# Sliding-window attention: 36 groups on 128-key blocks against 16 batches of 64-key blocks on smaller array tiles

## The chip, the cores and the metric

One core of one Trainium2 chip. The time is that of one execution on the device, in microseconds (us). Single durations are from profiled executions. All comparisons are between runs of the normal ("fast") state.

The engines: PE is TensorE (matmuls), PEld its weight loads, ACT is ScalarE, DVE is VectorE, POOL is GpSimd, SP the engine that issues the transfers. "L358" is line 358 of a kernel's file. PSUM is the memory that matmuls write to, in banks. A tile of the array is the part of its rows and columns that one matmul uses ("32*64" in the views); to change the tiling is to go on with tiles of another shape. A pair is a matmul with its weight load. The granted clock is the share of its full rate at which PE was let run.

## The reference

Two attention blocks over the same 2048 x 1024 input, 32 heads of 32, mixed by a gate. Block A is linear attention and is not touched. Block B lets each query see 8 keys, two positions apart:

```python
W, dil = 8, 2
idx = pos[:, None] - off[None, :]           # off = 0, 2, 4 .. 14
mask = idx >= 0
logits = jnp.einsum("bhsd,bhswd->bhsw", q, kg) * scale
logits = jnp.where(mask[None, None, :, :], logits, -1e9)
attn = _softmax(logits, axis=-1)
o = jnp.einsum("bhsw,bhswd->bhsd", attn, vg)
...
return g * a + (1 - g) * b
```

The kernels split positions into even and odd ("parity"), so that the 8 keys of a query are neighbours. A block of keys then serves a run of queries, with a band mask on exponentiated scores.

## The kernel before

PE's order is fixed by hand. In the attention stage the units of a long stream are the K and Q projections of block B (512-column matmuls, eight to a PSUM bank), and attention groups are dropped between them. Four tiles of 128 keys by 112 (or 128) queries, four heads each, make one group. There are 36 groups.

```python
def kq_units(c, kqt):
    ...                                     # 8 matmuls into a bank of ps_pj (2 banks), then its copy:
        after = (64 * c + 16 * b + 8 * which + 8 - 67) % (512 / 36)
        (nc.vector.tensor_copy if 0 <= after < 4 else nc.scalar.copy)(
            out=kqt[:, which, cols], in_=st["pj"][:])

def scores(g):                              # 16 matmuls, 32 rows x 128 columns of the array each
    for c, t, q0, w, k0 in tiles:
        for i in range(4):
            r = slice(32 * i, 32 * i + 32)
            nc.tensor.matmul(s4[:, i, o:o + w], lhsT=kqts[c][r, 0, k0:k0 + P],
                             rhs=kqts[c][r, 1, q0:q0 + w], start=True, stop=True)
    ...                                     # exponential on ACT, mask product on DVE, in two halves

def pv(g):                                  # 16 matmuls on the whole array, 33 columns (V and a 1)
    for b in range(2):
        for i in range(4):
            for tt in range(2 * b, 2 * b + 2):
                nc.tensor.matmul(oB[b][:, tt - 2 * b, i, :], lhsT=pt[:, i * W_ + o:i * W_ + o + P],
                                 rhs=V[:, t, c * 4 + i, :], start=True, stop=True)
    ...                                     # reciprocal, product on DVE; transposed by DMA
# cut: groups are placed every 512/36 units; pv 18 units after its scores
```

Note the choice in `kq_units`: the projection copy that falls just after a score group goes to DVE, because ACT then has two long exponentials to do.

The softmax here doesn't subtract the row's maximum and nothing guards it: scores larger than these inputs give would overflow.

## Time and profile before

| | before |
|---|---|
| median of the runs given first | 487.87 us (487.74 to 490.22) |
| PE busy, share of the span | 99% |
| attention stage, first projection matmul to first output matmul | 153.46 us |
| of it the 576 projection matmuls at 0.2157 us | 124.24 us |
| the rest: what attention costs PE | 29.2 us |

The last rows come from the start times of the matmuls in the trace. First, busy time per engine and the chain that ended last, from the page of the kernel before:

```profile
PE 480.5 (99%) x3444; PEld 227.0 (47%) x3444; DVE 281.0 (58%) x533; ACT 187.4 (39%) x283; POOL 15.9 (3%) x33
...
PE 98%; DMA 1%; SPq 1%; ACT 0%; issue 0%; ACTq 0%
PE kq_ps L339 23%; PE d_ps L454 21%; PE p_ps L258 11%; PE g_ps L200 11%; PE pk_ps L152 11%; PE p_ps L296 9%; PE q_ps L296 3%; PE oB L390 3%; PE s L365 2%; PE q_ps L454 1%; DMA WkA<-in_A_wqkv_dram 1%; PE kv_ps L220 0%; PE p_ps L246 0%; SPq L95 0%; SPq L98 0%; SPq L99 0%
```

A chain that is 98% PE says that only PE time counts: whatever ACT or DVE saves is worth nothing unless PE waits for them. Attention itself (oB and s) is only about 5% of the chain.

One group in the timeline of PE, kernel before (start, duration, engine, line, operation, output<-input, array rows*columns, count):

```profile
301.78 0.81 PE L339 MATMUL kq_ps<-xT,WkB 128*128 128x512 bf16 x3
302.52 0.38 PE L365 MATMUL s<-kqt 32*128 32x128 bf16 x16
302.83 1.04 PE L339 MATMUL kq_ps<-xT,WkB 128*128 128x512 bf16 x4
303.71 0.56 PE L390 MATMUL oB<-V,PT 128*128 128x33 bf16 x16
304.12 0.38 PE L339 MATMUL kq_ps<-xT,WkB 128*128 128x512 bf16 x1
```

Durations overlap, so read the starts. In the trace the last projection matmul before the scores starts at 302.209. A next one would follow 0.216 later, but the first score matmul comes at 302.520: 0.095 us lost. 15 more starts follow, then 0.14 us pass before the projections go on. PV needs no such pauses: 16 starts, 25.3 ns apart, 0.405 us.

### The profile page before, as it was taken

The page shows a single profiled execution, that of the slowest core. Times are in us where ns is not written, and L with a number is a line of the kernel's source. Part 1 is how long each engine was busy: PE and PEld are TensorE (multiplying, and loading weights), DVE is VectorE, ACT ScalarE, POOL GpSimd, SP SyncE. Part 2 cuts the span into 40 slices and gives each one's busy share as a digit, 9 for nine tenths or more (in the row PEclk, how much of TensorE's full clock was granted, in tenths as well). Part 3 has the DMA queues.
Part 4 walks back from the last instruction along what each step waited for, and adds up shares of the span by engine and source line. Part 5 has one row for each costly group of instructions (what it writes and reads, how often), then busy time and mean ns, then how long its engine had stood idle before and what let it go on. Part 6 is the DMA issues. An engine that isn't in the chain of part 4 may idle for free.

```text
span 486.2 us, 8390 instructions
## 1 busy us (share of the span) xinstructions
PE 480.5 (99%) x3444; PEld 227.0 (47%) x3444; DVE 281.0 (58%) x533; ACT 187.4 (39%) x283; POOL 15.9 (3%) x33
## 2 busy tenths in 40 slices
PE   7999999999999999999999999999999999999997
PEld 4444444445444444444444445544445444444444
DVE  1766689992429999995466556656654596000000
ACT  1333321111633333332666666666565332212121
POOL 3000001411000000000000000000000000000000
PEclk9999999999999999999999999999999999999999
DMA  8999960001522223354011161111173833111101
GB/s 194 171 291 369 348 207 0 0 1 36 190 76 93 72 71 93 95 158 131 11 30 31 30 121 27 38 30 32 31 172 78 198 88 86 34 43 34 43 33 45
DMA packets 80182, 46.57 MB, mean 96 GB/s; under 512 B 53520, under 2 KB 74128, under 8 KB 80144
## 3 DMA queue, kind: packets, MB, share of 16 engines
q1 hardware_dynamic: 80144, 46.04, 34.9%
q8 instruction: 27, 0.44, 0.4%
q14 instruction: 11, 0.09, 0.1%
HBM read 21.23 MB, written 7.34 MB: 59 GB/s over the span
## 4 chain that ended last, share of the span: by engine, by line
PE 98%; DMA 1%; SPq 1%; ACT 0%; issue 0%; ACTq 0%
PE kq_ps L339 23%; PE d_ps L454 21%; PE p_ps L258 11%; PE g_ps L200 11%; PE pk_ps L152 11%; PE p_ps L296 9%; PE q_ps L296 3%; PE oB L390 3%; PE s L365 2%; PE q_ps L454 1%; DMA WkA<-in_A_wqkv_dram 1%; PE kv_ps L220 0%; PE p_ps L246 0%; SPq L95 0%; SPq L98 0%; SPq L99 0%
## 5 line engine op out<-in xcount | busy, mean ns | idle before, releaser
L375 ACT ACTIVATE PT<-s 128x896 bf16<-128x896 f32 (+1 forms) x72 | 63.0, 926 | 24.5 <-PE s L365 24.5
L339 PE MATMUL kq_ps<-xT,WkB 128*128 128x512 bf16 x256 | 65.3, 379 | 0.0
L339 PE MATMUL kq_ps<-xT,WqB 128*128 128x512 bf16 x256 | 64.8, 379 | 0.0
L376 DVE TENSOR_TENSOR PT<-PT,mask 128x896 bf16<-128x896 bf16 (+1 forms) x72 | 44.6, 623 | 26.6 <-ACT PT L375 26.6
L258 PE MATMUL p_ps<-WvB,xT 128*128 128x512 bf16 x256 | 57.9, 379 | 0.0
L152 PE MATMUL pk_ps<-WkA,xT 128*128 128x512 bf16 x256 | 56.0, 379 | 1.3 <-DMA WkA<-in_A_wqkv_dram 0.8
L454 PE MATMUL d_ps<-WoA,pqT 128*128 128x512 bf16 (+1 forms) x248 | 56.9, 372 | 0.0
L454 PE MATMUL d_ps<-WoB,OBT 128*128 128x512 bf16 (+1 forms) x248 | 56.9, 372 | 0.0
L200 PE MATMUL g_ps<-pk,xrow 128*128 128x512 bf16 x256 | 55.4, 379 | 0.0
L140 DVE TENSOR_SCALAR e<-e 128x512 f32<-128x512 f32 x64 | 28.1, 438 | 41.8 <-ACT e L139 41.8
L459 ACT ACTIVATE osb<-d_ps,omg 128x512 bf16<-128x512 f32 (+1 forms) x31 | 20.9, 673 | 76.5 <-PE d_ps L454 73.7
L296 PE MATMUL p_ps<-WqA,xT 128*128 128x512 bf16 x192 | 43.4, 379 | 0.0
L344 ACT CAST kqt<-kq_ps 128x512 bf16<-128x512 f32 x48 | 28.2, 587 | 31.8 <-PE kq_ps L339 31.6
L152 PEld LDWEIGHTS <-xT 128*128 128x128 bf16 x256 | 24.9, 98 | 32.2 <-issue 1.6
L454 PEld LDWEIGHTS <-pqT 128*128 128x128 bf16 x264 | 25.8, 98 | 29.5
L454 PEld LDWEIGHTS <-OBT 128*128 128x128 bf16 x264 | 25.8, 98 | 29.3
L200 PEld LDWEIGHTS <-xrow 128*128 128x128 bf16 x256 | 25.0, 98 | 30.2
L258 PEld LDWEIGHTS <-xT 128*128 128x128 bf16 x256 | 24.6, 98 | 30.0 <-issue 0.9
L296 PEld LDWEIGHTS <-xT 128*128 128x128 bf16 x256 | 24.3, 98 | 28.5
L139 ACT ACTIVATE e<-pk_ps 128x512 f32<-128x512 f32 x32 | 19.0, 597 | 42.0 <-PE pk_ps L152 42.0
L339 PEld LDWEIGHTS <-WqB 128*128 128x128 bf16 x256 | 22.9, 97 | 24.7
L339 PEld LDWEIGHTS <-WkB 128*128 128x128 bf16 x256 | 22.6, 97 | 24.1
(56 smaller groups left out, 394.1 us busy)
## 6 DMA issues: line engine op xcount, KB each, us to landing
xrow<-in_A_x_dram SPq DMA_DIRECT2D x4, 1024.0 KB, 12.3
out_dram<-osb SPq DMA_DIRECT2D x31, 128.0 KB, 1.9
pqd<-tmp SPq DMA_DIRECT2D x12, 256.0 KB, 2.0
WvA<-in_A_wqkv_dram SPq DMA_DIRECT2D x2, 1024.0 KB, 15.0
WoA<-in_A_wo_dram SPq DMA_DIRECT2D x2, 1024.0 KB, 12.7
WvB<-in_B_wqkv_dram SPq DMA_DIRECT2D x2, 1024.0 KB, 12.5
WqA<-in_A_wqkv_dram SPq DMA_DIRECT2D x2, 1024.0 KB, 9.7
WkB<-in_B_wqkv_dram SPq DMA_DIRECT2D x2, 1024.0 KB, 6.6
```

Source lines behind the costliest of these rows:

```text
L139: nc.scalar.activation(out=e[:], in_=pj[:], func=ACT.Exp)
L140: nc.vector.tensor_scalar(out=e[:], in0=e[:], scalar1=1.0, scalar2=1e-6, op0=ALU.min, op1=ALU.add)
L152: nc.tensor.matmul(pj[:], lhsT=xT[:, kt, t * P:(t + 1) * P], rhs=WkA[half][:, kt, :], start=(kt == 0), stop=(kt == KT - 1))
L200: nc.tensor.matmul(pj[:], lhsT=xrow[:, t, kt * P:(kt + 1) * P], rhs=pk[:, t, half * 512:(half + 1) * 512], start=(t == 0), stop=(t == NB - 1))
L258: nc.tensor.matmul(st["pj"][:], lhsT=xT[:, kt, t * P:(t + 1) * P], rhs=WvB[half][:, kt, :], start=(kt == 0), stop=(kt == KT - 1))
L296: nc.tensor.matmul(st["pj"][:], lhsT=xT[:, kt, t * P:(t + 1) * P], rhs=WqA[half][:, kt, :], start=(kt == 0), stop=(kt == KT - 1))
L339: nc.tensor.matmul(st["pj"][:], lhsT=W[c // 4][:, kt, (c % 4) * P:(c % 4 + 1) * P], rhs=xT[:, kt, cols], start=(kt == 0), stop=(kt == KT - 1))
L344: (nc.vector.tensor_copy if 0 <= after < 4 else nc.scalar.copy)(out=kqt[:, which, cols], in_=st["pj"][:])
L375: nc.scalar.activation(out=ptv[:, hs], in_=s4[:, hs, 0:W_], func=ACT.Exp, scale=SCALE)
L376: nc.vector.tensor_tensor(out=ptv[:, hs], in0=ptv[:, hs], in1=m[:, None, :].broadcast_to([P, 2, W_]), op=ALU.mult)
L454: nc.tensor.matmul(st["ps"][:, 0:n], lhsT=lhsT, rhs=W[c0 // 512][:, c, c0 % 512:c0 % 512 + n], start=(side == 0 and c == 0), stop=(side == ...
L459: nc.scalar.activation(out=osb[:, 0:n], in_=st["ps"][:, 0:n], func=ACT.Copy, scale=omg[:, tb:tb + 1])
```

## The change

The intent: fewer, larger groups, so that fewer changes of the array's tiling are paid; blocks of 64 keys waste less; two parities share the partitions; PV's output is already transposed, so the 60 DMA transposes go. V travels through DRAM to be laid out by blocks. Denominators come from matmuls with ones, and DVE transposes them back and forth to divide. The core of the diff:

```diff
-                        after = (64 * c + 16 * b + 8 * which + 8 - 67) % (512 / 36)
-                        (nc.vector.tensor_copy if 0 <= after < 4 else nc.scalar.copy)(
-                            out=kqt[:, which, cols], in_=st["pj"][:])
-                for b in range(4):
+                        nc.scalar.copy(out=kqt[:, which, cols], in_=st["pj"][:])
+                for b in (0, 2, 1, 3):
...
+            def scores(c, run):
+                for q0, w, k0 in BLOCKS[9 * run:9 * run + 9]:        # 9 blocks, w = 56 to 64
+                    for par in range(2):
+                        for i in range(4):
+                            nc.tensor.matmul(s4[64 * par:64 * par + 64, i, o:o + w],
+                                             lhsT=kqts[c][r, 0, 1024 * par + k0:1024 * par + k0 + 64],
+                                             rhs=kqts[c][r, 1, 1024 * par + q0:1024 * par + q0 + w], ...)
...
+            def pv(c, run):
+                for m in range(9 * run, 9 * run + 9):
+                    for i in range(4):
+                        for par in range(2):
+                            r = slice(64 * par, 64 * par + 64)
+                            nc.tensor.matmul(o2[32 * i:32 * i + 32, par, o:o + w],
+                                             lhsT=V[r, m, c * P + 32 * i:c * P + 32 * i + 32],
+                                             rhs=pt[r, i, o:o + w], start=True, stop=True)
+                for i in range(4):
+                    for par in range(2):
+                        nc.tensor.matmul(den[32 * i:32 * i + 32, par, :], lhsT=onesb[r, 0:32], rhs=pt[r, i, :], ...)
+                # cut: DVE transposes den, takes reciprocals of one column, transposes back, multiplies
...
+                    p_ = 64 * c + 32 * run + 32 + 6
+                    events.append((p_, lambda c=c, run=run: scores(c, run)))
+                    events.append((p_ + 16, lambda c=c, run=run: pv(c, run)))
```

So a batch is one group of 72 score matmuls and, 16 projection matmuls later, one of 72 PV and 8 denominator matmuls. Each matmul has its weight load: 144 and 160 PE instructions in a row. There are 16 batches.

## The prediction

> **What bounds it now.** TensorE. The chain of waits that ended last is 98% PE, the granted clock is 1.000, and in the timeline the 128x512 matmuls start every 0.216 us without a hole from 9 us to the end. The change touches PE only inside attention (218 to 373 us).
>
> **PE cost of attention now** (start-to-start in the timeline). 36 score groups: 0.095 us extra before the first matmul, 15 gaps summing to 0.156 us, 0.140 us after the last: 0.391 us each, 14.1 us. 36 PV groups of 16 matmuls at 25.3 ns: 0.405 us each, 14.5 us. Together 28.6 us.
>
> **PE cost after.** 16 batches: 72 score matmuls of about 57 columns (eight tiles per block), 72 PV matmuls, 8 denominator matmuls of 512 columns. The 0.093 to 0.1 us on each side of score, KV and WoA groups is a change of array tiling; the Trainium skill, "TensorEngine Tiling (Array Packing)", Key Properties, says that such a change drains the engine, and the trace agrees. Before only scores pay it (36 pairs); after, scores and PV both do (32 pairs). Within a group, matmuls on different tiles start 3 to 4 ns apart here (the skill's "TensorE: Matmul & The Clock Gate", Part 3, says about 4), and a 64-column tile repeats every 31.6 ns (KV, L220). Estimate: a block of eight takes 31 ns; scores 0.095+8x0.031+0.117 = 0.46 us, PV with denominators 0.093+9x0.030+0.24+0.10 = 0.70 us; 16 x 1.16 = 18.6 us. Gain 10.0 us.
>
> **What the gain runs into.** Every projection copy in attention now goes to ScalarE; before, those that fall just after a score group went to VectorE. Scores are issued two units before a projection group ends, so its copy stands in ScalarE's order behind two 128x1024 exponentials. From before: 0.24 us from last score matmul to exponential, exponentials 0.92 us apart at this width (scaled from 0.81 at 896 and 0.84 at 928), copy 0.59: the bank is free 2.7 us after the last score matmul. PE wants it (double-buffered, ten units later) after 0.117+10x0.2157 = 2.27 us. Estimate: PE waits 0.45 us in each batch, 16 times: 7.3 us lost.
>
> **Off the path.** VectorE: per batch two mask products (0.7), two denominator transposes (0.65, estimated from the other 512-column PSUM operations), reciprocals, two transposes, two products: about 6 of 8.7 us, so it keeps up and PV finds its weights ready. 36 transpose DMA groups disappear; V goes through DRAM, about 4 MB more, in a stretch where DMA is a third busy; PV's V arrives before 231 us. GpSimd's mask building is early.
>
> **Sum.** 487.9 - 10.0 + 7.3 = 485.2; plus about 1.3 for the chance that PE cannot be fed 144 and 160 instructions at 2 ns each (the longest run seen, KV: 256 at 7.9 ns). **Predicted 486.5 us, 8 in 10 between 479 and 499. Faster by over 2%: 0.10; within 2%: 0.72; slower: 0.18.**
>
> **Signs.** Right: PE waiting for ScalarE's copy of the projection bank, 16 times, about 0.45 us each; score matmuls 4 ns apart on average; no PE wait for PT, V or the denominators' bank; VectorE about 65% busy in attention.
>
> **What would make it wrong.** No wait at the copy: about 478. Matmuls 8 ns apart or more once PE's queue runs dry: 0.3 us more in each of 32 groups, about 496. VectorE transposes at twice the estimate: PV would wait for the mask products. V late: one stall at the first PV.

## The result, and the profile after

| | before | after |
|---|---|---|
| median, four runs each | 488.5 us (487.74 to 490.22) | 496.44 us (495.35 to 496.6) |
| ratio of fast runs | 1 | 1.0156 (95%: 1.0132 to 1.018) |
| attention stage in the profile | 153.5 us | 160.9 us |
| what attention costs PE above the projections | 29.2 us | 36.6 us |
| DVE busy in the stage | 92 us | 92 us |
| ACT busy in the stage | 94 us | 70 us |

Ratios here and below are the mean time of one kernel's fast runs over that of the other's fast runs of the same rounds, so not quite the ratio of the medians quoted. The kernel became 1.6% slower, inside the predicted range and class, but 9.9 us above the central value. The attention stage accounts for 7.4 us of the 8.6 us between the two profiled runs (7.9 between the medians). Outside this stage the two profiles differ by 1.2 us net: a start 1.8 us longer, which varies from run to run (last experiment; in this profile of the changed kernel the granted clock was at half for 3.4 us there), and an end 0.6 us shorter. The busy times of the stage are from these two windows, kernel before first:

```profile
218.00:372.00 154.00, 154.00 (x1716) 75.42 (x1715) 92.30 (x240) 94.08 (x128) 0.00 (x0) 1.00 0.27 59
220.00:381.00 161.00, 151.40 (x2978) 74.92 (x3009) 92.05 (x171) 69.97 (x104) 0.00 (x0) 1.00 0.19 49
```

(Window, its length, then busy time of PE, PEld, DVE, ACT and POOL, the granted clock, and DMA.)

Busy time and chain of the changed kernel:

```profile
PE 477.4 (96%) x4661; PEld 226.8 (46%) x4724; DVE 276.7 (56%) x461; ACT 163.0 (33%) x259; POOL 22.9 (5%) x78
...
PE 89%; ACT 7%; issue 2%; DMA 1%; SPq 0%; ACTq 0%
PE d_ps L446 21%; PE kq_ps L338 16%; PE pk_ps L146 11%; PE p_ps L263 11%; PE g_ps L194 11%; PE p_ps L298 8%; ACT PT L365 6%; PE s L358 2%; PE q_ps L298 2%; PE o L380 2%; ACT kqt L341 1%; PE q_ps L446 1%; DMA xT<-in_A_x_dram 1%; PE den L386 1%; PE kv_ps L214 0%
```

ACT is now on the chain, with 7%. The chain in order of time shows how, for one batch (start, duration, what):

```profile
265.16 0.21 PE kq_ps L338
265.37 0.75 PE s L358 x72
266.12 0.02 issue
266.14 1.94 ACT PT L365 x2
268.08 0.49 ACT kqt L341
268.57 0.04 issue
268.61 1.46 PE kq_ps L338 x6
270.07 0.67 PE o L380 x72
270.74 0.26 PE den L386 x8
271.00 0.16 issue
271.16 3.40 PE kq_ps L338 x15
```

The chain goes from the scores through two exponentials and one projection copy back to PE. That ACT spell is on the chain does not mean that all of it is lost: PE works meanwhile. What is lost shows in PE's own timeline of the same batch:

```profile
265.31 0.77 PE L358 MATMUL s<-kqt 32*64 32x64 bf16 x72
266.23 0.38 PE L338 MATMUL kq_ps<-xT,WkB 128*128 128x512 bf16 x1 [0.16 <-issue]
266.45 1.89 PE L338 MATMUL kq_ps<-xT,WqB 128*128 128x512 bf16 x8
268.61 1.46 PE L338 MATMUL kq_ps<-xT,WkB 128*128 128x512 bf16 x6 [0.27 <-ACT kqt L341]
270.00 0.74 PE L380 MATMUL o<-PT,V 64*32 64x64 bf16 x72
270.56 0.44 PE L386 MATMUL den<-PT,onesb 64*32 64x512 bf16 x8
271.16 0.38 PE L338 MATMUL kq_ps<-xT,WkB 128*128 128x512 bf16 x1 [0.16 <-issue]
```

The idle time in brackets understates the wait, because it is counted from the modelled end of the last matmul. Starts say more: the gap at 268.61 is 0.653 us from start to start where 0.216 is normal, so 0.437 us are lost. The record of the first projection matmul after each group is missing (its weight load is there), hence the apparent 0.16 us of "issue"; the sums below allow for it. Per batch, from starts (us above the projections' own time):

| per batch | predicted | measured | as |
|---|---|---|---|
| scores | 0.46 | 0.80 | 0.093 + 0.563 + 0.148 |
| PV and denominators | 0.70 | 1.04 | 0.093 + 0.617 + 0.327 |
| wait for the copy | 0.45 | 0.44 | 0.653 - 0.216 |
| sum, times 16 | 25.9 | 36.4 | |

The wait is right; both groups cost 0.34 us more than predicted. The single starts of the score group at 265.305 show why. These are gaps from start to start in ns:

```
matmuls  1..32:  3 3 4 3 3 4 3 29 3 4 3 3 4 3 3 9 3 3 4 3 3 4 3 8 4 3 3 4 3 3 4
then one gap of: 99
matmuls 33..72:  8 9 8 8 9 8 8 9 8 8 9 8 8 9 ...   (8.3 on average, to the end)
```

32 matmuls start nearly as predicted, then comes a pause of 0.1 us, and the rest come 8.3 ns apart. The PV group does the same. Two questions follow: is the 0.437 us wait what I took it for, and what are the pause and the 8.3 ns?

### The profile page after: what moved, and what is told of

Same layout as the page of the kernel before. It is cut to its first block, busy times and chain, and to the rows that moved or that the text cites. A ratio compares the mean times of both kernels' runs of the same rounds, so it can differ in the third digit from the quotient of the medians.

```text
span 494.8 us, 10641 instructions
## 1 busy us (share of the span) xinstructions
PE 477.4 (96%) x4661; PEld 226.8 (46%) x4724; DVE 276.7 (56%) x461; ACT 163.0 (33%) x259; POOL 22.9 (5%) x78
## 4 chain that ended last, share of the span: by engine, by line
PE 89%; ACT 7%; issue 2%; DMA 1%; SPq 0%; ACTq 0%
PE d_ps L446 21%; PE kq_ps L338 16%; PE pk_ps L146 11%; PE p_ps L263 11%; PE g_ps L194 11%; PE p_ps L298 8%; ACT PT L365 6%; PE s L358 2%; PE q_ps L298 2%; PE o L380 2%; ACT kqt L341 1%; PE q_ps L446 1%; DMA xT<-in_A_x_dram 1%; PE den L386 1%; PE kv_ps L214 0%
## 5 line engine op out<-in xcount | busy, mean ns | idle before, releaser
L338 PE MATMUL kq_ps<-xT,WkB 128*128 128x512 bf16 x226 | 58.9, 379 | 9.0 <-issue 4.8
L338 PE MATMUL kq_ps<-xT,WqB 128*128 128x512 bf16 x256 | 60.5, 379 | 0.0
L146 PE MATMUL pk_ps<-WkA,xT 128*128 128x512 bf16 x251 | 57.1, 387 | 2.1 <-DMA WkA<-in_A_wqkv_dram 1.1
L341 ACT CAST kqt<-kq_ps 128x512 bf16<-128x512 f32 x64 | 36.2, 595 | 59.5 <-PE kq_ps L338 59.5
L146 PEld LDWEIGHTS <-xT 128*128 128x128 bf16 x256 | 25.4, 100 | 33.5 <-issue 3.8
L391 DVE STREAM_TRANSPOSE dT<-den 128x512 f32<-128x512 f32 x32 | 21.0, 695 | 35.3 <-PE den L386 35.3
L446 PEld LDWEIGHTS <-OBT 128*128 128x128 bf16 x264 | 25.8, 98 | 29.4
L338 PEld LDWEIGHTS <-WqB 128*128 128x128 bf16 x256 | 25.1, 98 | 30.2
L298 PEld LDWEIGHTS <-xT 128*128 128x128 bf16 x256 | 24.9, 98 | 30.4 <-issue 0.8
L365 ACT ACTIVATE PT<-s 128x1024 bf16<-128x1024 f32 x32 | 31.0, 1021 | 23.2 <-PE s L358 23.2
L263 PEld LDWEIGHTS <-xT 128*128 128x128 bf16 x256 | 24.6, 98 | 30.0 <-issue 0.9
L366 DVE TENSOR_TENSOR PT<-PT,mask 128x1024 bf16<-128x1024 bf16 x32 | 22.0, 691 | 26.4 <-ACT PT L365 26.4
```

The lines of the kernel that those rows point to most:

```text
L146: nc.tensor.matmul(pj[:], lhsT=xT[:, kt, t * P:(t + 1) * P], rhs=WkA[half][:, kt, :], start=(kt == 0), stop=(kt == KT - 1))
L263: nc.tensor.matmul(st["pj"][:], lhsT=xT[:, kt, t * P:(t + 1) * P], rhs=WvB[half][:, kt, :], start=(kt == 0), stop=(kt == KT - 1))
L298: nc.tensor.matmul(st["pj"][:], lhsT=xT[:, kt, t * P:(t + 1) * P], rhs=WqA[half][:, kt, :], start=(kt == 0), stop=(kt == KT - 1))
L338: nc.tensor.matmul(st["pj"][:], lhsT=W[c // 4][:, kt, (c % 4) * P:(c % 4 + 1) * P], rhs=xT[:, kt, cols], start=(kt == 0), stop=(kt == KT - 1))
L341: nc.scalar.copy(out=kqt[:, which, cols], in_=st["pj"][:])
L365: nc.scalar.activation(out=pt[:, hs], in_=s4[:, hs], func=ACT.Exp, scale=SCALE)
```

## The experiments

### 1. One copy per batch to DVE

```diff
-                        nc.scalar.copy(out=kqt[:, which, cols], in_=st["pj"][:])
+                        (nc.vector.tensor_copy if b < 2 and which == 0 else nc.scalar.copy)(
+                            out=kqt[:, which, cols], in_=st["pj"][:])
```

(and the same for the one such copy in the last batch, which falls in another projection).

> The changed kernel with one projection copy per batch (the one that ends just after the scores) moved from ScalarE to VectorE. Theory (the copy stands behind two exponentials and PE waits 0.437 us for the bank in each of 16 batches): these waits vanish, the gap between the two matmuls falls from 0.653 to 0.216 us, and the kernel gains 16 x 0.437 = 7.0 us, to about 489.4 us. Rival (ScalarE or the bank is short over the whole batch, so the wait only moves): waits of a similar size appear at a later bank or at PV, gain under 3 us.

Measured: 489.53 us (489.38 to 490.49), ratio to before 1.0017 (0.9996 to 1.0038). The attention stage costs PE 30.5 us above the projections, against 36.6. The timeline of PE where the wait was:

```profile
264.45 0.38 PE L338 MATMUL kq_ps<-xT,WkB 128*128 128x512 bf16 x1 [0.16 <-issue]
264.67 1.89 PE L338 MATMUL kq_ps<-xT,WqB 128*128 128x512 bf16 x8
266.39 1.46 PE L338 MATMUL kq_ps<-xT,WkB 128*128 128x512 bf16 x6
267.78 0.74 PE L381 MATMUL o<-PT,V 64*32 64x64 bf16 x72
```

From 264.67 eight matmuls at 0.2157 us end at 266.39, exactly where the next group starts: no gap. PE's waits for copies over the whole run, by name (total, times, longest), first in the changed kernel, then here:

```profile
PE kq_ps L338 <- ACT kqt L341: 4.2, 15, 0.4
```

```profile
PE kq_ps L338 <- DVE kqt L341: 0.6, 2, 0.3
```

(These sums understate too: by starts the waits are 7.1 us in 16 batches, the last of them under another tile's name, and here 0.9 us in two places early in the stage.) The theory of the wait stands, and its size too: 6.1 us less in the stage, 6.9 us less in the medians. The rival, a wait that only moves, falls.

### 2. Each tile used again after four matmuls

```diff
-                for q0, w, k0 in BLOCKS[9 * run:9 * run + 9]:
-                    for par in range(2):
+                for par in range(2):
+                    for q0, w, k0 in BLOCKS[9 * run:9 * run + 9]:
```

> The changed kernel with the score matmuls in another order: first all blocks of one parity, then the other, so that each array tile is used again after 4 matmuls, not 8. Same instructions, same columns. Supply theory (PE's instruction queue holds 64 instructions; once these are used up, an instruction arrives every 4.2 ns, 8.3 ns for each weight load with its matmul): the score group stays at 0.56 us from first to last start, total unchanged within 1 us. Tile theory (each visit to a tile needs 66 ns for load and stream, eight tiles give 8.3 ns): four tiles give 16.6 ns each, the group takes about 1.1 us, the kernel is 8 to 9 us slower.

Measured: 495.72 us (494.76 to 496.3), ratio 1.0137. The score group takes 0.580 us from first to last start, against 0.563; the exit after it is shorter by the same, and the attention stage is 160.87 us in both. The 8.3 ns are not what a tile needs between visits: each tile is now used again after 33 ns, not 66, at the same pace.

```profile
265.10 0.77 PE L358 MATMUL s<-kqt 32*64 32x64 bf16 x72
```

What a tile does need shows in the first 32 starts of this run. They come in fours, 3 or 4 ns apart, with mostly 22 ns to the next four, so a tile was used again after about 32 ns.

### 3. Twice the instructions for the same columns

Each score matmul was split into two of half the columns.

> The changed kernel with each score matmul split into two of half the columns (28 or 29), so 144 weight loads and matmuls for the same streamed columns. Supply theory: 72 more pairs at 8.3 ns, 0.60 us more in each of 16 batches, 9.6 us slower; starts 4 ns apart for the first 32 and 8.3 ns after. Column theory (time follows the columns streamed): score groups stay at 0.56 us, total unchanged within 1 us.

Measured: 513.67 us (512.38 to 514.91), ratio 1.0506. The score group takes 1.150 us, against 0.563: 0.587 us for 72 more pairs, 8.2 ns each. Again 32 start quickly, then a pause, then 8.3 ns. Time follows the number of instructions, not the columns. Nor does the width of the weight load set it: in the changed kernel a score pair loads 64 columns and a PV pair 32, and both come 8.3 ns apart. The instructions explain 9.4 of 17.2 us; the other 7.8 us are longer waits a few projection matmuls after each score group, which the profile puts down to no releaser. In these 17 places the lost time sums to 15.0 us, against 7.1 us of waits for the copy in the changed kernel. One such place, by the timeline of PE:

```profile
266.99 1.34 PE L360 MATMUL s<-kqt 32*64 32x32 bf16 x144
268.49 0.38 PE L338 MATMUL kq_ps<-xT,WkB 128*128 128x512 bf16 x1 [0.16 <-issue]
268.71 0.59 PE L338 MATMUL kq_ps<-xT,WqB 128*128 128x512 bf16 x2
269.86 0.38 PE L338 MATMUL kq_ps<-xT,WqB 128*128 128x512 bf16 x1 [0.56 <-issue]
```

The DMA records of this trace point to the cause. Its page has this line:

```profile
q8 instruction: 46, 0.75, 0.6%
```

These are transfers of 16 KB, one for every 256 instructions of PE and PEld: 46 for 11689 here, 37 for 9385 in the changed kernel, 27 for 6888 in the kernel before. In 16 of the 17 places PE goes on 1.3 to 1.6 us after such a transfer has ended, although 0.56 to 1.80 us are lost. At the waits for the copy in the changed kernel the same distance is anything from 0.2 to 5.3 us. So PE very probably waited here for its own instructions to be brought. That is read from one trace; no run was made to test it.

### 4. Groups small enough to be held ready

```diff
+                    for third in range(3):
+                        events.append((p_ + 2 * third, ...scores(c, run, third)))   # 3 blocks each
+                    events.append((p_ + 20, lambda c=c, run=run: pv(c, run)))
```

> On top of copy_dve (489.5 us), each batch of 72 score matmuls in three groups of 24 (48 instructions) with two projection matmuls between, and PV four units later. Supply theory: each group fits in the 64 instructions held ready, so there is no pause after the 32nd matmul and starts are 4 ns apart on average throughout; but each group pays the change of tiling: 0.093 + about 0.095 + 0.12 = 0.31 us, three times 0.31 = 0.92 us against 0.80 us now, so 16 x 0.12 = 1.9 us slower, about 491.4 us. Rival (8.3 ns is an average that the array reaches by the column or tile): groups of 24 take 24/72 of 0.563 us, 0.19 us each, and the kernel is about 6 us slower.

Measured: 492.68 us (491.36 to 493.7), ratio to before 1.0087. Each group of 24 takes 0.108 us from first to last start (4.7 ns per start), with no pause anywhere; with 0.093 before and 0.121 after, three groups cost 0.97 us against 0.80 for one of 72. The stage is 2.6 us dearer than in copy_dve, where 1.9 were expected. So within 48 instructions the quick rate holds, and the change of tiling, paid twice more, eats more than that saves.

### 5. Denominators in the middle, and split: two misses

If PE's queue refills while 512-column matmuls stream, these should stand in the middle of PV, not at its end, where their streaming is a tail of 0.33 us.

```diff
+                    if m - 9 * run != 3:
+                        continue
+                    for i in range(4):                    # denominators after the fourth block
+                        for par in range(2):
```

> The changed kernel with the eight 512-column denominator matmuls after the fourth of nine PV blocks, not after the ninth. Supply theory: PE's queue fills up again while these eight stream for 0.21 us, the next 32 matmuls start 4 ns apart, and the tail after the last start is 0.13 and not 0.33 us: first PV start to next projection matmul falls from 0.94 to about 0.71 us, the kernel gains 3 to 4 us. Tile or array theory (8.3 ns is what the array needs for a matmul): the starts stay 8.3 ns apart, the denominators still occupy the tiles for 0.2 us, the total is unchanged or up to 2 us slower.

Measured: 496.13 us (495.0 to 496.5), ratio 1.0145: a gain of 0.3 us in the stage, not 3 to 4. The tail did shrink (to 0.14 us). But the next matmul on a tile had to wait until its denominator matmul had streamed (the hold of a tile: 0.215 us from start to start here), and after this hold only some 24 matmuls came quickly, then another pause of 0.06 us. Next, an order in which no tile is held:

```diff
+                for par in range(2):
+                    # 4 denominator matmuls of the other parity, then 36 PV matmuls of this one
```

> On top of copy_dve (489.5 us), PV in another order, same instructions: the four denominator matmuls of parity 1 first, then the 36 PV matmuls of parity 0, the four denominator matmuls of parity 0, then the 36 PV matmuls of parity 1. No tile is wanted again while it streams 512 columns. Supply theory in the form that den_middle left (a group of 160 instructions lasts as long as their supply, about 0.62 us from first to last start, and whatever holds the engine on top is lost): nothing is held, and the tail from the last start to the next projection matmul falls from 0.33 to about 0.13 us; 0.19 us less in each of 16 batches, 3.1 us, to about 486.4 us, below the kernel before. Rival (a queue effect that makes any order cost the same 0.92 to 0.94 us from first PV start to the next projection matmul, as den_middle showed): 489 to 490 us.

Measured: 492.39 us (491.4 to 495.02), ratio to before 1.0091: 2.6 us dearer in the stage than copy_dve, not 3.1 cheaper. The pause before matmul 32 (counted from 0) had grown from 0.11 to 0.20 us, and there was one of 0.15 us before matmul 72. Supply alone does not explain this.

The starts and (modelled) ends of these groups do. Take the group of copy_split at 260.478, in ns from its first start:

```
matmul  0 (denominator)  starts   0,  ends 386      matmul 32 starts 413
matmul 40 (denominator)  starts 484,  ends 863      matmul 72 starts 890
```

And in the changed kernel matmul 0 (PV) ends at about 200, and matmul 32 starts at 226. I took the smallest value of "start of matmul k+32 minus end of matmul k" over all groups of each kernel: it is 26 or 27 ns in every one, and it is met at nearly every pause over 45 ns that is not the hold of a tile (four single ones are left over). So, as far as modelled ends can tell, no more than 32 pairs are under way at a time, and a pair counts until its matmul has ended. A 512-column matmul takes 0.38 us and blocks its place that long. That is the window theory. It was made from these traces, so it needed a forecast.

### 6. Forecasts of the window theory

On top of copy_dve, denominators after five, six or seven of the nine blocks.

> On top of copy_dve: the eight denominator matmuls after five PV blocks (matmuls 40 to 47 of 80). Window theory: denominators at 0.29 to 0.35 us after the first PV start, matmul 48 held until 0.51; then a second pause, at matmul 72 (40 + 32) and nowhere else, until the first denominator matmul has ended (0.39 us after its start), 0.69 to 0.71 us; last start at about 0.76, next projection matmul at about 0.89 us. 0.05 us less than copy_dve in 16 batches, 0.9 us, to about 488.6 us, and 0.9 us slower than copy_den6. Rival (supply alone, no window to the end of a matmul): no pause at matmul 72, the same time as copy_den6.

Measured: 489.43 us (488.39 to 490.67), ratio to before 1.0016. A pause of 0.07 us stands before matmul 72 in 15 of 16 groups, and otherwise only those before matmul 32 and, by the tile that is held, before 48. The next weight load came at 0.90 us (0.93 in copy_dve), where 0.89 was expected. The stage costs 0.3 us less than in copy_dve, not 0.9: the PV groups give 0.5, and one early wait for a copy is 0.3 longer. The place of the pause is right; the gain was too high.

> On top of copy_dve (489.5 us): the eight denominator matmuls after six PV blocks (matmuls 48 to 55 of 80). New theory, formed from the earlier traces (window theory): 64 instructions, 32 load and matmul pairs, may be under way until they have ended, so matmul k+32 starts no earlier than 26 ns after the end of matmul k; beyond that a pair is supplied every 8.3 ns; and a tile that streams 512 columns is held for 0.213 us. It forecasts: pause before matmul 32 until 0.226 us; denominators at 0.36 to 0.42; matmul 56 held until 0.57; from there about 18 starts 4 ns apart and six 8.3 ns apart, no pause at 64 or 72; last start at 0.70, next projection matmul (its weight load) at about 0.83 us after the first PV start, against 0.94 now. 0.11 us less in 16 batches: 1.8 us, to about 487.7 us. Rival (what den_middle and copy_split showed is that any order costs 0.92 us or more): 489.5 us or more.

Measured: median 488.28 us, but the profiled run took 1302 us: a disturbed execution in which even the projection matmuls came mostly 0.62 us apart and not 0.216, at a granted clock of 1.000. One run of the kernel before took 2386 us. These two are left out; the five other runs give a ratio of 0.9987 (0.9963 to 1.0011). Without a usable profile the forecast could not be checked, so the kernel was run again.

> The same kernel as copy_den6, whose profile fell into a run of 1302 us and cannot be used. Window theory with the hold as copy_den5 measured it (0.223 us from a tile's denominator matmul to its next): matmul 56 at about 0.58 us after the first PV start, no pause at 64 or 72, last start at about 0.72, next projection matmul at about 0.85 us against 0.94 in copy_dve: 1.5 us less in all, about 488.0 us. Rival: 0.92 us or more, 489.5 us.

Measured: 488.23 us (487.33 to 489.12), ratio 1.0002 (0.9988 to 1.0016). No pause stands at 64 or 72 in any group. The stage costs PE 28.4 us above the projections: 2.1 less than copy_dve (1.5 expected) and 0.8 less than the kernel before. The timeline of its PV group, then that of copy_den5:

```profile
267.30 0.55 PE L381 MATMUL o<-PT,V 64*32 64x64 bf16 x48
267.66 0.44 PE L389 MATMUL den<-PT,onesb 64*32 64x512 bf16 x8
267.88 0.29 PE L381 MATMUL o<-PT,V 64*32 64x56 bf16 x24
```

```profile
267.03 0.48 PE L381 MATMUL o<-PT,V 64*32 64x64 bf16 x40
267.32 0.44 PE L389 MATMUL den<-PT,onesb 64*32 64x512 bf16 x8
267.55 0.45 PE L381 MATMUL o<-PT,V 64*32 64x56 bf16 x32
```

The last part has 24 matmuls in 0.29 us here, and 32 in 0.45 us there: eight more, and the pause. The 24 start 4.8 ns apart on average, on the tiles that the matmuls before the hold used 8.3 ns apart. So 8.3 ns is not the least that the array needs; pairs that had time to gather during the hold go faster.

> On top of copy_dve: the denominators after seven PV blocks (matmuls 56 to 63 of 80). Window theory: no matmul stands 32 behind a denominator, so no pause after the one before matmul 32; matmul 64 held until about 0.65 us, the last 16 by then all supplied and 4 ns apart, last start at about 0.71, next projection matmul at about 0.84 us: within 0.3 us of copy_den6 in all, about 487.9 us. Rival: 489.5 us.

Measured: 488.84 us (487.57 to 489.65), ratio 1.0009; no pause but those at 32 and at the held tile, as forecast. The stage costs 29.4 us, 1.0 more than copy_den6, where 0.3 was the limit. The next weight load came at 0.85 us (0.84 expected), but at 0.81 in copy_den6 (0.85 expected), which makes 0.6 us; the other 0.4 us are a longer early wait for a copy.

### 7. The masks, and the start

> copy_den6 with the 72 mask selects on GpSimd moved from the first 20 us to after the KV stage, to see whether they cause the slower start. In the profiles the attention stage of copy_den6 costs TensorE 0.8 us less than that of the kernel before (28.4 against 29.2 us above the projections' own time), yet the total is the same, because the first projection stage lost 1 to 2 us more to late loads and a half clock. If the selects cause this: about 487.3 us, below the kernel before by 0.2%, and the granted clock is 1.000 in nearly all runs. If the start varies by chance of the transfers: 488.2 us as before, with 0.997 in a part of the runs.

Measured: 488.04 us (487.11 to 488.87) against 488.73 of before in the same rounds, ratio 0.9979 (0.9963 to 0.9995). The stage costs 28.5 us. Two of six runs still have the lower granted clock (0.996), so it comes without the early selects too. The kernel before shows 0.997 too, in 3 of 7 runs on one chip, and these took 489.6 us where the others took 487.8 to 488.6. The profiles show where the start differs: the ninth projection matmul starts at 8.7 us in the kernel before and at 10.1 us in den6_mask, which waits longer for the load of WkA (2.2 us against 0.8) and runs at half the clock for 3.4 us around that time. By what chance is open, and no run of the kernel before was profiled in that state. This version is nominally the quickest of all, by 0.2%: by the 2% rule, the same.

## Why the prediction was right or wrong

- **PE is the bound; only its time in attention counts.** Right: 7.4 of the 8.6 us between the profiles are in that stage.
- **PE waits for a copy behind two exponentials, 0.45 us in each batch.** Right, and shown: 0.437 us measured, gone when the copy moved to DVE, 6.1 us less in the stage.
- **DVE keeps up; V and the masks are in time.** Right: 92 of 161 us busy in the stage (57%, where 65% was expected), and no wait of PE for PT or for V is listed. The transposes took 0.695 and 0.673 us; 0.65 was the estimate.
- **Scores 0.46 us and PV 0.70 us in a batch.** Wrong: 0.80 and 1.04. The failed step is the term "a block of eight takes 31 ns" (30 for PV): it held for four blocks, and the rest took 66 ns each after a pause of 0.1 us. The sign "score matmuls 4 ns apart on average" failed with it, at 7.9 ns. Together 16 x 0.68 = 10.9 us, all of the miss in the sum. The rate of 3 to 4 ns was read from groups of 16 matmuls, 32 instructions, and carried over to groups of 144 and 160. The only long group in the trace, KV with 256, ran at 7.9 ns an instruction, and I read it as the need of its tiles. That reading was right, and for that reason KV could not give warning: its pairs start 3 and 28 ns apart in turn, 15.9 on average, because two tiles are each used every 32 ns. A stream slower than 8.3 ns a pair does not show how fast pairs can come.
- **What would make it wrong: "8 ns apart or more once PE's queue runs dry ... about 496".** That is what happened, with the size given. It had been weighted with only 1.3 us in the sum.
- **The gain of 10.0 us in PE time.** There was none: without the 7.1 us of waits attention costs PE 29.5 us after, against 29.2 before (estimated at 28.6, because a score group costs 0.40 us and not 0.39). The changes of tiling fell only from 36 groups with one on each side to 32, while the pairs of weight load and matmul doubled from 1152 to 2432.
- **Within 2%.** The class held, but not for the reason given. The forecast set a gain of 10.0 us against waits of 7.3; the run had no gain and 7.1 us of waits. That 1.6% still fell inside is in part luck.

What remains open: what sets the 8.3 ns for a pair after the first 32 (experiments 2 and 3 exclude tile visits and columns, and copy_den6 shows the array going faster; instruction supply fits, but was not measured by itself), a test of the waits of experiment 3, and the chance in the start.

## What to carry to other kernels

Count instructions, not only columns: on small array tiles the first 32 pairs of a group are nearly free, then each costs 8.3 ns here, even at half the columns. A score group took 0.56 us from first to last start, where the prediction had 0.25. A long matmul inside such a group holds its place until it ends: put it where no matmul stands 32 behind it. And when an evacuation is moved to another engine's queue, look at what stands ahead of it there; one copy per batch behind two exponentials cost 6 to 7 us in all.

## What the Trainium skill lacked or had wrong

- "TensorE: Matmul & The Clock Gate", table at the top, gives PE a queue of 64 instructions. It does not say that a place is held until the matmul has ended: in all groups here matmul k+32 started at least 26 ns after the modelled end of matmul k.
- The same page, Part 3, gives a span of one matmul plus about 4 ns for each further tile. This held for the first 32 pairs of a group (3 to 4 ns, with small pauses). The page's table ends at 16 tiles and it does not say what follows in a longer group: here 8.3 ns for each pair.
- The same page, Part 1, says that start to start never drops below about 25 ns. That fits the PV matmuls of the kernel before on the whole array (25.3 ns), but on different tiles starts were 3 to 4 ns apart, nearer to Part 3 of the page.
- "TensorEngine Tiling (Array Packing)", Key Properties, says that a change of tiling mode drains the engine, without a size: here 0.093 us before a group, and 0.12 to 0.15 us from the last start of a short-column group to the next projection.
- No page gives the length of a wait of PE for its own instructions in straight code: if the reading of experiment 3 is right, 0.56 to 1.80 us in 16 places there.
